# Reordered feed-forward units and sums in a fused attention and mixer kernel

## The chip, the cores and the metric

The kernel runs on one core of one Trainium2 chip. The metric is the device time of one execution in microseconds. The core has five engines with a queue each, all in order: TensorE (PE; its weight loads are PEld), VectorE (DVE), ScalarE (ACT), GpSimd (POOL) and SyncE (SP, which here only issues DMAs). Semaphores tie them together: an instruction that waits holds up all that stands behind it on its engine.

## The reference

The input is four batches of 8 heads, 768 positions and 64 channels. The attention keeps the first 8 positions and a band of 96, with a linear bias by distance; a low-rank token mixer and a feed-forward network follow.

```python
scores = scale * np.matmul(q, k.transpose(0, 1, 3, 2)) + bias        # band of 96 and 8 global columns kept
a = softmax(np.where(keep, scores, -1e9))
x = np.matmul(a, v).transpose(0, 2, 1, 3).reshape(B, S, H * D)       # 4 x 768 x 512
xt = x.transpose(0, 2, 1)
u = x + (xt @ U @ V).transpose(0, 2, 1)                              # U 768 x 32, V 32 x 768
return u + np.maximum(u @ w_ch1, 0.0) @ w_ch2                        # w_ch1 512 x 2048, w_ch2 2048 x 512
```

## The kernel before

**Attention blocks.** A block `i` handles two heads of one batch: batch `i // 4`, head pair `i % 4`, blocks 0 to 15. Its steps are the scores in three parts (`scores`, L366 and L373; `s_dve` adds the bias on VectorE, L406 and L412, into the single buffer `sp`), two exponentials on ScalarE (`st_E`, L430) and the product with v for each of the two heads (`st_V`, TensorE L443 and L447 into the one bank `ob`, then reciprocal L452 and normalisation L466 on VectorE, then a cast to `x16` on GpSimd, L469). From block 7 on the second and third score parts are computed together ("S12"); the first two use the single two-bank tile `sc`, the third takes two of the three `th` banks. A block's steps for the mixer come one block later: `st_M1` (x by U, L478), `st_MT` (L495, copied by VectorE to `tmp16`, L496), `st_M3` (L532 into `sc`, added to `x_sb` by VectorE, L537, cast by GpSimd, L540) and `st_X`, a DMA transpose on SP's queue that gives a quarter of `uT` (L521).

**Feed-forward units.** A batch has three groups of 256 tokens, each two tiles of 128. An *up unit* is eight matmuls of u by w_ch1 (L646) into a `th` bank and a ReLU on ScalarE (L651). For batch 0 a *down unit* is a quarter of one token tile's product with w_ch2: `mk_down(t, part)`, four matmuls (L681) into a `cps` bank (two banks in all, shared with the products below). Quarter `part` reads rows `4 * part` to `4 * part + 3` of `w2_16`, which are chunk `part` of four loads issued on GpSimd's queue (L230). The first quarter of a tile also adds the low-rank term (L675), the last is followed by the add to `x_sb` on VectorE (L686) and the store, which batch 0 keeps for later. For batches 1 to 3 a group of two tiles is done with seven products of half size in place of eight (`mk_product`, x1 to x4 and y1 to y3, L699, add L704). They need sums: of quarters of w_ch2 (t1 to t4, made once) and of quarters of the ReLU output (s1 to s4, in two halves `k` per group), all of them L570 on VectorE.

**The order.** Everything is in an order written out by hand. From block 4 on, each block has nine places (counted 0 to 8) at which `fill(n)` puts `n` units between the attention steps; the order of one block is: first scores, place 0, V of the block before (first head), place 1, S12, place 2, V (second head), second score part's bias add, place 3 (two units from block 8 on, and in some earlier ones), place 4, M1 and the first exponential, place 5, MT, place 6, M3 and the second exponential, place 7, the `uT` transpose, place 8. `unit` takes ups and downs in turn from the two queues `ups_q` and `downs_q`; while `held` is true no down unit is taken. All 24 up units of batch 0 come before any down unit.

**The sums.** `queue_sum` puts a sum with a due count into `jobs` (s) or `slow` (t). After each unit `fill` takes out one sum that is due (two, if more than four s sums are waiting). `queue_weight_sums` queues the t sums when tile 1 of group 0 begins. A product whose sums aren't out yet takes them out by force (`need`).

Of the kernel before, what the change touches and what calls it, by code (L numbers as in the profile page):

```python
# [20 lines left out]
def kernel(  # L21
# [17 lines left out]
    P = 128  # L39
# [4 lines left out]
    NJC = DFF // P  # L44
    R = moe_U.shape[1]
    NP = H // 2
# [40 lines left out]
    def ps_cps(name):  # L87
        return psum.tile([P, 512], FP32, name=name, tag="cps", bufs=2)

    def ps_th(name, dtype=FP32, cols=512):  # L90
        return psum.tile([P, cols], dtype, name=name, tag="th", bufs=3)
# [26 lines left out]
    def cast_qk(i, *engs):  # L118
        got = []
        for st, nm, eng in zip(staged.pop(i), ("q16", "k16"), engs * 2):  # L120
            st16 = stp.tile([P, NSB, 2, D], FP16, name=nm, tag=nm, bufs=2)
            turn_over = eng.copy if eng is nc.scalar else eng.tensor_copy
            turn_over(st16.rearrange("p n h d -> p h n d"), st)
            got.append(st16)
        cast[i] = got
# [78 lines left out]
    v16w = cst.tile([P, S], FP16, name="v16w")  # L204
# [337 lines left out]
    ups_q, downs_q = deque(), deque()  # L542
# [20 lines left out]
    jobs, slow = deque(), deque()  # L563
# [3 lines left out]
    def queue_sum(name, part, out_, a, b_, op, wait=0):  # L567

        def go():
            nc.vector.tensor_tensor(out_, a, b_, op)  # L570
            have.add((name, part))
        (slow if name[0] == "t" else jobs).append((count[0] + wait, go))
# [25 lines left out]
    def weight(w, j):  # L598
        return tw[w][:, j] if w != "t3" else tw[w][j // 2][:, j % 2]
# [11 lines left out]
    def queue_group(b, g):  # L611
        ts = slice(g * FT, (g + 1) * FT)
        uT, tmp16, x_sb = uTs[b], tmps[b], xs[b]
        n0, n1 = 2 * g, 2 * g + 1
        cell = {}

        split = (b, g) in WG
        follow = (b, g + 1) if g + 1 < NFG else (b + 1, 0)
        last = (b, g) == (B - 1, NFG - 1)

        def queue_sums(k):

            h = cell["htr"]
            if k == 0:
                for x in (1, 2, 4):
                    cell[f"s{x}"] = ffp.tile([P, HJ, P], FP16, name=f"s{x}", tag=f"s{x}", bufs=1)
                cell.update(a11=h[:, 0:HJ, 0:P], a12=h[:, HJ:NJC, 0:P],
                            a21=h[:, 0:HJ, P:FT], s3=h[:, 0:HJ, P:FT], a22=h[:, HJ:NJC, P:FT])
            js = slice(k * HJ // 2, (k + 1) * HJ // 2)
            for name, a, b_, op in (  # L630
                ("s1", "a21", "a22", ALU.add), ("s2", "s1", "a11", ALU.subtract),
                ("s4", "a12", "s2", ALU.subtract), ("s3", "a11", "a21", ALU.subtract),
            ):
                queue_sum((name, b, g), k, cell[name][:, js], cell[a][:, js], cell[b_][:, js], op, wait=0 if last else 2)

        def mk_up(at):
            jp = at // 2 + (at % 2) * NJC // 4 if split else at

            def go():
                if jp == 0:  # L640
                    cell["htr"] = ffp.tile([P, NJC, FT], FP16, name="htr", tag="htr", bufs=3)
                hps, done = begun.pop(jp) if jp in begun else (ps_th("hps"), 0)
                for k in range(2):
                    jt = 2 * jp + k
                    for dc in range(done, NDC):
                        nc.tensor.matmul(  # L646
                            hps[:, k * FT:(k + 1) * FT],
                            w1_16[:, dc, jt * P:(jt + 1) * P], uT[:, dc, ts],
                            start=(dc == 0 and k == 0), stop=(dc == NDC - 1 and k == 1),
                        )  # L650
                nc.scalar.activation(  # L651
                    cell["htr"][:, 2 * jp:2 * jp + 2].rearrange("p j t -> p (j t)"), hps, AF.Relu
                )
                if split and at % 4 == 3:
                    queue_sums(at // 4)
            return go

        def store(n, cs=slice(0, DM)):
            def go():
                nc.sync.dma_start(out[b, n * P:(n + 1) * P, cs], x_sb[:, n, cs])  # L660
            if b:
                go()
            else:
                kept.append(go)

        def mk_down(t, part):
            n = 2 * g + t

            def go():
                if (b, g, t, part) == (0, 0, 1, 0):  # L670
                    queue_weight_sums()
                if part == 0:
                    cell["cps"] = ps_cps("cps")
                    if b == 0:
                        nc.tensor.matmul(  # L675
                            cell["cps"], v16w[:, n * P:(n + 1) * P], tmp16,
                            start=True, stop=False,
                        )
                cps, htr = cell["cps"], cell["htr"]
                for jc in range(4 * part, 4 * part + 4):  # L680
                    nc.tensor.matmul(  # L681
                        cps, htr[:, jc, t * P:(t + 1) * P], w2_16[:, jc],
                        start=(b > 0 and jc == 0), stop=(jc == NJC - 1),
                    )
                if part == NJC // 4 - 1:
                    nc.vector.tensor_tensor(x_sb[:, n], cps, x_sb[:, n], ALU.add)  # L686
                    store(n)
            return go

        def mk_product(bank, half, a, w, dst, first=False, done=None):  # L690

            def go():
                if bank not in cell:
                    cell[bank] = ps_cps(bank)
                need(*(((a, b, g), k) for k in range(2) if a[0] == "s"))
                need(*((w, k) for k in range(4 if w == "t3" else 2) if w[0] == "t"))
                ps = cell[bank][:, half]
                for j in range(HJ):
                    nc.tensor.matmul(  # L699
                        ps, cell[a][:, j], weight(w, j), start=(first and j == 0),  # L700
                        stop=(done is not None and j == HJ - 1), skip_group_check=True,
                    )
                n, cs = dst
                nc.vector.tensor_tensor(x_sb[:, n, cs], ps, x_sb[:, n, cs], ALU.add)  # L704
                for what in done or ():
                    store(*what)
            return go

        if b:
            for at in range(NJC // 2):  # L710
                ups_q.append((mk_up(at), (b, g)))
        else:
            first_ups.append([(mk_up(at), (b, g)) for at in range(NJC // 2)])
        if split:
            x1 = mk_product("cx", lo, "a11", "b11", (n0, lo), first=True)
            x2 = mk_product("cx", lo, "s2", "t2", (n0, hi_))
            x3 = mk_product("cx", lo, "s3", "t3", (n1, hi_), done=[(n1, hi_)] if last else None)
            x4 = mk_product("cx", lo, "a22", "t4", (n1, lo), done=[(n1, lo)] if last else [(n1,)])
            y1 = mk_product("cy", lo, "a12", "b21", (n0, lo), first=True)
            y2 = mk_product("cy", hi_, "s1", "t1", (n1, hi_))  # L720
            y3 = mk_product("cy", hi_, "s4", "b22", (n0, hi_), done=[(n0,)])
            for made in (x1, y1, x2, y2, x3, y3, x4):
                downs_q.append((made, (b, g)))
        else:
            for t in range(2):
                for part in range(NJC // 4):
                    downs_q.append((mk_down(t, part), (b, g)))

    ahead, held, kept = [0], [True], deque()

    def fill(n):
        for _ in range(n):
            unit()
            count[0] += 1
            for _ in range(2 if len(jobs) > 4 else 1):
                for queue in (jobs, slow):
                    if queue and queue[0][0] < count[0]:
                        queue.popleft()[1]()
                        break
# [79 lines left out]
    for i in range(NP, NPAIR + 2):  # L819
        b, hp = divmod(i, NP)  # L820
        live = i < NPAIR
        units = iter(
            (0, 1, 1, 2, 1, 1, 1, 1, 1) if i == NP
            else (0, 1, 1, 1, 1, 1, 1, 1, 1) if i + 1 < NPE
            else (1, 1, 1, 2, 1, 1, 1, 1, 1)
        )
# [62 lines left out]
        if live:  # L889
            st_E(i, 0)  # L890
            if i < NPE:
                st_P(i)
        fill(next(units))
        if i >= NPE:
            for _ in range(min(2, len(kept))):
                kept.popleft()()
# [14 lines left out]
            st_X(i - 1)  # L911
        if NPE <= i + 2 < NPE + 2:
            cast_qk(i + 2, nc.gpsimd)
        fill(next(units))
    while ups_q or downs_q:
        fill(1)
# [36 lines left out]
```

## Time and profile before

| | |
|---|---|
| median of 3 runs | 233.32 us (231.82 to 234.01) |
| the profiled execution | 231.37 us |
| its span, first to last instruction | 229.6 us |
| mean granted TensorE clock | 0.998 |
| TensorE busy | 219.3 us (96%) |
| VectorE busy | 158.6 us (69%) |
| ScalarE busy | 125.9 us (55%) |
| GpSimd busy | 70.7 us (31%) |
| L646, up matmuls | 756 x 273 ns |
| L681, down matmuls of batch 0 | 96 x 379 ns |
| L570, weight sums of 128x1024 | 6, most of them 0.68 us |
| w loads, issue to landing | 8.6 us median |

Times in the trace are counted from the start of the span. A matmul's row shows its duration with the pipeline's fill and drain, so that one matmul's time overlaps the next one's: eight L646 matmuls of 273 ns take 0.87 us together. A line of the timeline shows start, duration, engine, line, operation, what it writes and reads, shape and count; what stands in brackets is the idle time of the engine before it, and what ended it. A line of the waits shows who waited for whom, total us, times, and the longest. A window's row shows, for PE, PEld, DVE, ACT and POOL in this order, busy us and the number of instructions, then granted clock and DMA.

### The profile page before, as it was taken

The numbers are of one execution on the slowest core, as the hardware profiler recorded it, in microseconds if no ns is written. First come the engines' busy times: TensorE is split into PE (matmuls) and PEld (weight loads), VectorE is DVE, ScalarE is ACT, GpSimd is POOL, SyncE is SP. The second block draws the span as 40 slices with busy tenths as digits, with TensorE's granted clock in tenths as the row PEclk, the third lists the DMA queues.
The fourth block names the chain that finished last, engine by engine and source line by source line (L and its number), as shares of the span: only waits on it lengthen the run. The fifth ranks groups of instructions, "written<-read, shape, count | busy, mean of one in ns | idle before, by whom it ended". The sixth has DMA issues, their size and how long they took to land.

```text
span 229.6 us, 5883 instructions
## 1 busy us (share of the span) xinstructions
PE 219.3 (96%) x2418; PEld 172.0 (75%) x2420; DVE 158.6 (69%) x346; ACT 125.9 (55%) x196; POOL 70.7 (31%) x115
## 2 busy tenths in 40 slices
PE   7889999999989999998999989999999999999993
PEld 2446678788644546886888868888989888888882
DVE  3688775749586979597979887979764444444452
ACT  6677857685705253958485847392732433333320
POOL 6398637297543423131313131313111000000000
PEclk9999999999999999999999999999999999999999
DMA  6999999989998979999999993751321202010022
GB/s 203 280 291 237 267 221 246 303 159 179 193 170 188 201 184 238 219 232 217 215 245 174 261 178 97 129 174 30 92 67 34 94 0 94 0 69 26 8 86 93
DMA packets 86563, 36.68 MB, mean 160 GB/s; under 512 B 74152, under 2 KB 83592, under 8 KB 86536
## 3 DMA queue, kind: packets, MB, share of 16 engines
q1 hardware_dynamic: 81480, 32.01, 57.5%
q0 software_dynamic: 5056, 4.29, 12.5%
q8 instruction: 19, 0.31, 0.6%
q14 instruction: 8, 0.07, 0.1%
HBM read 27.46 MB, written 6.29 MB: 147 GB/s over the span
## 4 chain that ended last, share of the span: by engine, by line
PE 67%; DVE 11%; DMA 10%; ACT 5%; POOL 4%; issue 1%; SPq 1%; ACTq 0%
PE hps L646 25%; PE cx L699 13%; PE cy L699 10%; PE cps L681 8%; DMA w<-in_moe_w_ch_dram 6%; DMA vst<-in_v_dram 3%; DVE sp L412 3%; PE sc L366 2%; ACT ep L430 2%; PE ob L447 2%; DVE x_sb L466 1%; PE sc L532 1%; PE tp L254 1%; PE ob L443 1%; DVE x_sb L704 1%
## 5 line engine op out<-in xcount | busy, mean ns | idle before, releaser
L646 PE MATMUL hps<-uT,w 128*128 128x256 f16 x756 | 95.5, 273 | 0.2 <-ACT htr L651 0.2
L651 ACT ACTIVATE htr<-hps 128x512 f16<-128x512 f32 x96 | 56.4, 599 | 60.8 <-PE hps L646 60.6
L646 PEld LDWEIGHTS <-w 128*128 128x128 f16 x756 | 71.0, 98 | 9.6 <-issue 0.3
L412 DVE SCALAR_TENSOR_TENSOR sp<-sc,relcat 128x1024 f32<-128x1024 f32 (+1 forms) x27 | 32.1, 1189 | 8.0 <-ACT ep L430 4.3
L430 ACT ACTIVATE ep<-sp 128x1408 f16<-128x1408 f32 x24 | 33.2, 1383 | 0.0
L699 PEld LDWEIGHTS <-htr 128*128 128x128 f16 x288 | 27.7, 98 | 3.4
L704 DVE TENSOR_TENSOR x_sb<-cx,x_sb 128x256 f32<-128x256 f32 x36 | 15.2, 422 | 19.3 <-PE cx L699 18.6
L469 POOL CAST x<-x_sb 128x384 f16<-128x384 f32 x27 | 14.1, 522 | 46.6 <-DVE x_sb L466 43.6
L681 PE MATMUL cps<-w,htr 128*128 128x512 f16 x96 | 23.6, 379 | 1.1 <-DMA w<-in_moe_w_ch_dram 1.1
L540 POOL CAST x<-x_sb 128x768 f16<-128x768 f32 x12 | 11.0, 914 | 43.2 <-DVE x_sb L537 43.2
L699 PEld LDWEIGHTS <-s 128*128 128x128 f16 x216 | 20.2, 98 | 4.3 <-DVE s L570 2.0
L704 DVE TENSOR_TENSOR x_sb<-cy,x_sb 128x256 f32<-128x256 f32 x27 | 11.4, 422 | 12.5 <-PE cy L699 12.3
L466 DVE TENSOR_TENSOR x_sb<-ob,rcp 128x384 f32<-128x384 f32 x30 | 16.7, 558 | 1.0
L366 PEld LDWEIGHTS <-kT 64*128 64x128 f16 x192 | 8.5, 93 | 11.4 <-issue 10.1
L447 PE MATMUL ob<-v,ep 128*128 128x65 f16 x192 | 16.6, 193 | 0.0
L366 PE MATMUL sc<-qT,kT 64*128 64x128 f16 x192 | 15.7, 220 | 0.3 <-DVE x_sb L537 0.2
L681 PEld LDWEIGHTS <-htr 128*128 128x128 f16 x96 | 8.6, 97 | 9.4 <-issue 1.2
L447 PEld LDWEIGHTS <-ep 128*128 128x128 f16 x192 | 13.9, 98 | 2.3 <-issue 0.5
L443 PE MATMUL ob<-vA,ep 128*128 128x65 f16 x160 | 14.4, 194 | 0.4 <-DVE vA L316 0.2
L537 DVE TENSOR_TENSOR x_sb<-sc,x_sb 128x768 f32<-128x768 f32 x12 | 11.5, 956 | 4.6 <-PE sc L532 4.6
L142 POOL CAST v<-vst 128x768 f16<-128x768 f32 x16 | 13.4, 838 | 3.8 <-DMA vst<-in_v_dram 3.8
L373 PE MATMUL sc<-qT,kA 64*128 64x128 f16 x160 | 13.2, 216 | 0.3
(110 smaller groups left out, 320.1 us busy)
## 6 DMA issues: line engine op xcount, KB each, us to landing
qst<-in_q_dram SPq DMA_DIRECT2D x16, 384.0 KB, 5.4
kst<-in_k_dram SPq DMA_DIRECT2D x16, 384.0 KB, 6.4
vst<-in_v_dram SPq DMA_DIRECT2D x16, 384.0 KB, 4.1
out_dram<-x_sb SPq DMA_DIRECT2D x23, 256.0 KB, 3.3
w<-in_moe_w_ch_dram POOLq DMA_DIRECT2D x8, 512.0 KB, 8.6
vA<-v SPq DMA_DIRECT2D x8, 152.3 KB, 4.1
out_dram<-x_sb SPq DMA_DIRECT2D x2, 128.0 KB
uT<-x SPq DMA_TRANSPOSE x12, 3.1
```

Of the source, the lines that this page charges most:

```text
L366: nc.tensor.matmul(scs[hi][:, o:o + P], kT[r, kb * P:(kb + 1) * P], qT[r, kb * P:(kb + 1) * P], start=(o == 0 and not on_pe), stop=(o + P ...
L412: nc.vector.scalar_tensor_tensor(out=sps[i][:, :, c0:c0 + tot], in0=both[:, :, 0:tot], scalar=qk_scale / slope[2 * (i % NP)], in1=relfs[c0 ...
L430: nc.scalar.activation(eps[i][:, hi], sps[i][:, hi], AF.Exp, scale=slope[2 * (i % NP)])
L443: nc.tensor.matmul(ob[:, qi], ep[:, OF[qi - 1]:OF[qi - 1] + P], vA[:, qi - 1, hi], start=True, stop=False,)
L447: nc.tensor.matmul(ob[:, qi], ep[:, DG[qi]:DG[qi] + P], vt[:, qi, hi], start=(qi == 0), stop=True,)
L466: nc.vector.tensor_tensor(xo, ob[:, :, 0:D], rb, ALU.mult)
L469: nc.gpsimd.tensor_copy(x16, xo)
L646: nc.tensor.matmul(hps[:, k * FT:(k + 1) * FT], w1_16[:, dc, jt * P:(jt + 1) * P], uT[:, dc, ts], start=(dc == 0 and k == 0), stop=(dc == ...
L651: nc.scalar.activation(cell["htr"][:, 2 * jp:2 * jp + 2].rearrange("p j t -> p (j t)"), hps, AF.Relu)
L681: nc.tensor.matmul(cps, htr[:, jc, t * P:(t + 1) * P], w2_16[:, jc], start=(b > 0 and jc == 0), stop=(jc == NJC - 1),)
L699: nc.tensor.matmul(ps, cell[a][:, j], weight(w, j), start=(first and j == 0), stop=(done is not None and j == HJ - 1), skip_group_check=True,)
L704: nc.vector.tensor_tensor(x_sb[:, n, cs], ps, x_sb[:, n, cs], ALU.add)
```

## The change

- Token tiles of a group have an accumulator each (`cell[t]`), so that both can be open.
- In group (0, 0) the fourth quarters of both tiles are moved behind the third quarters of both: (0,0), (0,1), (0,2), (1,0), (1,1), (1,2), (0,3), (1,3) as (tile, quarter).
- `held` is cleared ahead of place 8 of block 6, not at the start of block 7.
- The second-half s sums (k = 1) are due one unit after they are queued, not two; those of the first half stay at two, and the last group's at none.
- From block 5 on, place 5 lets out no sum; the next unit may take out one more.

```diff
@@ queue_sums
-                queue_sum((name, b, g), k, ..., op, wait=0 if last else 2)
+                queue_sum((name, b, g), k, ..., op, wait=0 if last else 2 - k)
@@ mk_down
                 if part == 0:
-                    cell["cps"] = ps_cps("cps")
+                    cell[t] = ps_cps("cps")
                     if b == 0:
                         nc.tensor.matmul(
-                            cell["cps"], v16w[:, n * P:(n + 1) * P], tmp16,
+                            cell[t], v16w[:, n * P:(n + 1) * P], tmp16,
                             start=True, stop=False,
                         )
-                cps, htr = cell["cps"], cell["htr"]
+                cps, htr = cell[t], cell["htr"]
@@ queue_group
-            for t in range(2):
-                for part in range(NJC // 4):
-                    downs_q.append((mk_down(t, part), (b, g)))
+            order = [(t, part) for t in range(2) for part in range(NJC // 4)]
+            if (b, g) == (0, 0):
+                order.sort(key=lambda u: u[1] == NJC // 4 - 1)
+            for u in order:
+                downs_q.append((mk_down(*u), (b, g)))
@@ fill
-    def fill(n):
+    owed = [0]
+
+    def fill(n, quiet=False):
         for _ in range(n):
             unit()
             count[0] += 1
-            for _ in range(2 if len(jobs) > 4 else 1):
+            pops = owed[0] + (2 if len(jobs) > 4 else 1)
+            owed[0] = 1 if quiet else 0
+            for _ in range(0 if quiet else pops):
                 for queue in (jobs, slow):
                     if queue and queue[0][0] < count[0]:
                         queue.popleft()[1]()
@@ the loop over the blocks, place 5
-        fill(next(units))
+        fill(next(units), quiet=i > NP)
@@ the loop over the blocks, place 8
+        held[0] = i < NP + 2
         fill(next(units))
```

More of the change, by code (lines that the diff above doesn't have):

```diff
@@ L633, in queue_sums @@
             ):
-                queue_sum((name, b, g), k, cell[name][:, js], cell[a][:, js], cell[b_][:, js], op, wait=0 if last else 2)
+                queue_sum((name, b, g), k, cell[name][:, js], cell[a][:, js], cell[b_][:, js], op, wait=0 if last else 2 - k)
         def mk_up(at):
```

## The prediction

> **What bounds the kernel now.** Read the engine table first, then who TensorE waited for, then the timeline around each wait.
>
> ```profile
> span 229.6 us, 5883 instructions
> PE 219.3 (96%) x2418; PEld 172.0 (75%) x2420; DVE 158.6 (69%) x346; ACT 125.9 (55%) x196; POOL 70.7 (31%) x115
> ...
> PE cx L699 <- DVE s L570: 1.5, 2, 1.0
> ...
> PE cps L681 <- DMA w<-in_moe_w_ch_dram: 1.1, 1, 1.1
> ...
> PE sc L366 <- DVE x_sb L537: 0.2, 1, 0.2
> PE hps L646 <- ACT htr L651: 0.2, 1, 0.2
> ```
>
> TensorE is busy 219.3 of 229.6 us, and the change neither adds nor removes a matmul. It can win only what TensorE idles in the middle. The waits above (total, times, longest) are all there are between 33 us and the end, and the change touches the neighbourhood of each. The timeline puts them at 60.5, 66.2, 100.4, 104.2 and 137.6 us:
>
> ```profile
> 60.51 0.23 PE L366 MATMUL sc<-qT,kT 64*128 64x128 f16 x2 [0.17 <-DVE x_sb L537]
> ...
> 64.91 0.19 PE L447 MATMUL ob<-v,ep 128*128 128x65 f16 x1
> 66.21 1.02 PE L681 MATMUL cps<-w,htr 128*128 128x512 f16 x4 [1.12 <-DMA w<-in_moe_w_ch_dram]
> ...
> 136.01 0.60 PE L699 MATMUL cx<-t,s 128*128 128x256 f16 x4
> 137.56 0.61 PE L699 MATMUL cx<-t,s 128*128 128x256 f16 x4 [0.96 <-DVE s L570]
> ```
>
> Recorded idle understates the loss, because the drain of the last matmul counts as busy. From issue to issue: the V step before the weight wait issues its last matmul at 64.91 (0.03 each), the next starts at 66.21, so 1.27 is lost, not 1.12. The half product at 136.01 issues four matmuls at 0.109 (eight take 0.87 in the chain), is through at 136.45 and goes on at 137.56: 1.11. In the same way 60.51 costs 0.34 (the up unit from 59.30 is through at 60.17), 104.22 costs 0.65 (from 103.13 + 0.44) and 100.36 costs 0.34 (98.81 + 0.87 + 0.34 for V). **All five: 0.34 + 1.27 + 0.34 + 0.65 + 1.11 = 3.7 us.** That is the ceiling.
>
> **The change, part by part.** I write (i, k) for place k, counted from 0, of attention block i.
>
> *Down units one place sooner.* Walking the two queues by their rule, place (6, 8) is empty before: the 24 up units of batch 0 are done and downs are held. It now takes token tile 0's first quarter: 0.22 for L675 and 0.87 for four L681 matmuls, from 60.17 to 61.26. The scores behind it (L366) needed the L537 result, there at 60.46: that wait goes, gain 0.34. Every later unit stands one place earlier among the attention steps; the units' total is the same, so the tail after the last place loses one.
>
> *Third quarters before fourths.* Quarter q needs chunk q of w2. The issues at 48.01, 48.75, 51.03 and 51.69 landed 7.4, 10.7, 11.8 and 14.5 later: 55.4, 59.4, 62.8 and 66.2. The new order reaches quarters 0, 1, 2 of tile 0 at 60.4, 61.6 and 62.85 (61.26 + 0.38 scores + 0.87 + 0.34 V), so chunk 2 is there by a hair: cost 0, up to 0.3. Then scores 0.5, tile 1's quarter 0 (1.09), V (0.34) and quarters 1 and 2 (1.73) put the fourth quarter at 67.4, 1.2 after its chunk. Gain 1.27. The price is that both cps banks are open at once. Group 1's first unit, at 69.3, needs tile 0's bank, freed by the L686 add (0.69). VectorE reaches it at about 68.45 (two 0.65 weight sums, V's normalisation and the 1.13 score pass stand ahead) and is through at 69.14. Cost 0; if one more 0.65 sum stood ahead, 0.5.
>
> *Where the weight sums now fall.* They start at (7, 2), not (7, 3), so t2's first half stands on VectorE ahead of the residual add L537 of block 6:
>
> ```profile
> 71.76 0.95 DVE L537 TENSOR_TENSOR x_sb<-sc,x_sb 128x768 f32<-128x768 f32 x1
> 72.62 0.68 DVE L570 TENSOR_TENSOR t<-w,t 128x1024 f16<-128x1024 f16 x1
> ...
> L570 DVE TENSOR_TENSOR t<-w,t x4: 681/682/1100, 72.6 to 88.9; 128x1024 f16<-128x1024 f16 x4
> ...
> 86.54 1.28 SPq L521 DMA_TRANSPOSE uT<-x  x1
> ```
>
> That sum can't start before the kA copy, which waits for a transpose landing near 70.8; so the add runs 71.65 to 72.6, as before, while TensorE wants block 8's scores at 72.5 and they need the bank the add reads. Cost 0.2 (0 to 0.6).
>
> The slow sum, 1.10, ran from 74.97 beside Pool's k cast (74.71 to 75.53). The other three took 0.68. The Trainium skill, SBUF — State Buffer, "Who interferes with whom", says that a VectorE instruction with both inputs in SBUF contends with a GpSimd instruction that reads SBUF. By that rule the second t2 half, now due at about 72.5 beside Pool's x cast, would take 1.10 and leave a gain 0.4 smaller than the sum below; the trace agrees for the one pair, but the sum at 72.62 ran 0.68 although the cast began at 72.77. I take 0.68.
>
> *Batch 1's transposed input.* TensorE reaches the first batch-1 up unit at 89.92 now, and after at 89.92 - 1.6 (the two gains so far) + 0.2 = 88.5; I allow 0.2 for the gaps of a few hundredths between steps and say 88.3. Its fourth matmul (+0.33, 88.63) reads the L521 transpose above, issued at 86.54. Transposes of that line landed 3.1 after issue in the median, 4.3 at most. The transpose is the end of a chain: V of block 7, Pool's casts, SP's vA copies at 80.71, two loads, two stores. VectorE's backlog at that V is smaller after (tile 2's add and t2's second half are already out), and SP is free from 79.6, so the chain moves up by 1.1 to 85.45: landing 88.55. I take 0.1; with the slowest landing 1.1.
>
> *ReLU sums.* In block 10 the ups are a place earlier and the second-half sums are due one unit earlier (wait 2 - k). s2's second half is emitted at (10, 2), ahead of the second V and the 1.13 score pass, not behind them at (10, 3). The waits at 104.22 (0.65) and, since L651 of the last up now stands ahead of the k cast that waited for its load, at 100.36 (0.34) go. What is late next is the M1 matmul, which needs Pool's cast of V's output: margin about 0.1 after, 0.5 before. Cost 0.1 (0 to 0.5).
>
> In block 13 the product x2 moves up as well, to (13, 3) right behind V, so there is less time. Counting from block 13's first score: x1 is through at 2.42; on VectorE its add runs to 2.95, s1 to 3.28, two L406 passes to 4.25, y1's add to 4.6, s2 to 5.0. TensorE wants s2's second half at 4.68. Of 1.11 lost, 0.4 stays (0.2 to 0.8).
>
> *Quiet places.* Place 5 lets out no sum, the next one more: this keeps a 0.42 sum from standing ahead of the tmp cast (L496, 0.29) that M3 waits for. Nothing recorded waits there; 0. After block 17, units follow each other at 0.87 with sums of 0.42: no wait there before, none after. Stores for later tiles move one place up on SP, once past a transpose; its margin of 1.1 us covers one 0.7 issue.
>
> **Sum.** 3.7 - (0 + 0 + 0.2 + 0.1 + 0.1 + 0.4) = **2.9 us**. Extremes: all costs at the upper end (0.3 + 0.5 + 0.6 + 1.1 + 0.5 + 0.8 = 3.8) make it 0.1 slower; none makes it 3.7 faster. Against the profiled execution, 231.37 (span 229.6 and 1.77 around it, which stays), that is 228.5. The median of the runs shown is 233.32; I carry the difference over: 233.32 - 2.9 = **230.4**. The runs differ by 2.2 us among themselves; if it is late w2 chunks that do that, the gain there is much the same: with chunks 2 and 3 both 2 us late, the old order loses 3.3 and the new one 1.9 at quarter 2, after which quarter 3 is covered.
>
> **Rivals.**
> *The waits come back elsewhere (chance 0.26).* The same in-order VectorE feeds everything, and it is full:
>
> ```profile
> 73.40:84.60 11.20, 11.20 (x99) 5.69 (x99) 9.58 (x18) 4.89 (x6) 4.42 (x7) 1.00 0.87 191
> ...
> 95.80:107.00 11.20, 10.43 (x130) 8.70 (x130) 9.95 (x22) 8.69 (x14) 2.19 (x4) 1.00 0.96 223
> ```
>
> The third busy time is VectorE's: 86% and 89% of these blocks. With half of the upper ends of the costs (1.9) the gain is 1.8, with all it is nil: 231.5 to 233.5, within 1%. For it: three margins above are 0.1 or less. Against it: each is a different wait.
>
> *VectorE falls behind for good (chance 0.12).* The single ob bank ties V of one head to the normalisation of the other. If the earlier sums leave VectorE one weight sum (0.65) behind from block 7 on, TensorE waits that long in each of the blocks 7 to 15: nine times 0.65 is 5.9, less 3.7 is 2.2 slower, about 235.5. It decides from 0.41 per block (3.7 / 9). Against it: 1.6 and 1.25 us of slack per block in the two rows; a backlog of 0.65 is gone within one block.
>
> *The change doesn't do what it says*: chunk 3 later than 67.4, or x2 in block 13 no better. Losing either leaves 1.6 or 2.2 of gain; it lies in the first rival.
>
> **Numbers.** The forecast has the rest, 0.62. One per cent, 2.3 us, is about what a measurement of this kernel can tell from no change. The range runs from 228.2 (all 3.7, and 1.4 for the runs' own scatter) to 233.0 (most of the first rival) and leaves out the slower one. Faster by over 1% 0.62, within 1% 0.26, slower by over 1% 0.12.
>
> **What would show it.** After the change: no L681 wait on w, or one of under 0.3 at quarter 2; the first L681 near 60.4, ahead of the scores; t2 ahead of L537 near 71; a short wait of L366 on L537 near 72.5; no x2 wait in block 10 and one of 0.2 to 0.4 recorded in block 13. It is wrong if TensorE then waits for uT near 88.5 by over 1 us, or if VectorE's idle in blocks 8 to 12 disappears.

## The result and the profile after

The changed kernel takes 229.75 us in the median of 22 runs, the kernel before 231.11 in the median of 22 runs of its own; the ratio is 0.9942 with a 95% interval of 0.9921 to 0.9963. That is 1.3 us faster, 0.6%, and within the 1% that the prediction called no change. Five of the changed kernel's 22 executions ran at a granted clock of 0.993 or less (two of them, at 0.56 and 0.66, took 367 and 316 us) and are left out of the ratio. The forecast was 2.9 us, from 233.32 to 230.4, in a range of 228.2 to 233.0. That the time comes within 0.7 us of the forecast is luck: the three runs of the kernel before that the prediction started from were 2.2 us high, the gain was put 1.6 too large, and the two nearly cancel. From 231.11 the same sum gives 228.2 and a range of 226.0 to 230.8, which still holds 229.75.

The page of the changed kernel and who TensorE waited for (total us, times, longest):

```profile
span 227.8 us, 5878 instructions
PE 219.0 (96%) x2420; PEld 171.8 (75%) x2420; DVE 160.1 (70%) x346; ACT 125.7 (55%) x196; POOL 70.3 (31%) x115
...
PE hps L646 <- DMA uT<-x: 1.4, 2, 1.1
...
PE cx L699 <- DVE s L570: 0.2, 1, 0.2
...
PE sc L366 <- DVE x_sb L537: 0.2, 1, 0.2
PE cps L681 <- DMA w<-in_moe_w_ch_dram: 0.2, 1, 0.2
```

The waits on w (1.1) and on s (1.5 in total) are down to 0.2 each, and the one on L651 is gone. In their place stands one that the kernel before did not have: the up matmuls wait for `uT`. The timeline of the changed kernel places all of them:

```profile
62.43 1.02 PE L681 MATMUL cps<-w,htr 128*128 128x512 f16 x4 [0.17 <-DMA w<-in_moe_w_ch_dram]
...
72.50 0.23 PE L366 MATMUL sc<-qT,kT 64*128 64x128 f16 x2 [0.22 <-DVE x_sb L537]
...
88.24 0.49 PE L646 MATMUL hps<-uT,w 128*128 128x256 f16 x3
88.99 2.45 PE L646 MATMUL hps<-uT,w 128*128 128x256 f16 x21 [0.26 <-DMA uT<-x]
...
133.86 0.61 PE L699 MATMUL cx<-t,s 128*128 128x256 f16 x4 [0.24 <-DVE s L570]
134.30 0.49 PE L646 MATMUL hps<-uT,w 128*128 128x256 f16 x3
135.92 0.71 PE L646 MATMUL hps<-uT,w 128*128 128x256 f16 x5 [1.13 <-DMA uT<-x]
```

The 62.43 wait is quarter 2, the 72.50 wait block 8's first scores, 133.86 the product x2 of block 13. At 88.24 and at 134.30 three matmuls of the first up unit of a batch run, and the fourth, which reads the last quarter of `uT`, waits: 0.42 and 1.29 lost from issue to issue (the step to the fourth matmul less the 0.11 that one takes).

**How to compare two profiles here.** The start of the last batch-0 up unit, ahead of everything that the change moves, lies at 59.30 us in the profile before and at 58.51 in the one after: 0.8 of the 1.8 between the two spans comes from code that is the same. So the runs below are compared from that instruction (L646, 8 matmuls) to the last product (L699), which all kernels have. The way is cut in two at batch 1's first up unit; the last column is what the fourth up matmul of a batch lost to `uT` in the second part, from issue to issue:

| kernel | last batch-0 up | last product | from one to the other | up to batch 1 | from there | of it lost to `uT` |
|---|---|---|---|---|---|---|
| before | 59.30 | 224.89 | 165.6 | 30.62 | 134.97 | 0 |
| changed | 58.51 | 223.07 | 164.6 | 29.73 | 134.83 | 1.71 |
| changed, second profile | 58.90 | 223.59 | 164.7 | 29.12 | 135.57 | 2.69 |
| tile order alone | 59.22 | 224.55 | 165.3 | 30.38 | 134.95 | 0 |
| early place alone | 59.05 | 226.70 | 167.7 | 30.83 | 136.82 | 0.19 |
| sums alone | 58.17 | 223.60 | 165.4 | 30.42 | 135.01 | 0 |
| order and early place | 59.33 | 228.02 | 168.7 | 29.71 | 138.98 | 0.76 |
| changed, store of place 7 behind the transpose | 59.41 | 223.05 | 163.6 | 29.11 | 134.53 | 1.65 |
| changed, all stores behind | 59.26 | 221.26 | 162.0 | 29.11 | 132.89 | 0 |
| the same, second profile | 59.21 | 221.50 | 162.3 | 29.41 | 132.89 | 0 |
| changed, kept stores alone behind | 61.38 | 224.36 | 163.0 | 29.11 | 133.87 | 1.00 |
| changed, stores of places 5 to 7 alone behind | 64.03 | 226.29 | 162.3 | 29.11 | 133.16 | 0.27 |
| before, all stores behind | 57.96 | 223.31 | 165.4 | 30.39 | 134.96 | 0 |

The rows with stores moved belong to the second half of the experiments.

### The profile page after: what moved, and what is told of

It is laid out like the page before. It is cut to its first block, busy times and chain, and to the rows that moved or that the text cites. A ratio compares the mean times of both kernels' runs of the same rounds, so it can differ in the third digit from the quotient of the medians.

```text
span 227.8 us, 5878 instructions
## 1 busy us (share of the span) xinstructions
PE 219.0 (96%) x2420; PEld 171.8 (75%) x2420; DVE 160.1 (70%) x346; ACT 125.7 (55%) x196; POOL 70.3 (31%) x115
## 4 chain that ended last, share of the span: by engine, by line
PE 70%; DMA 12%; DVE 10%; POOL 3%; ACT 2%; issue 2%; SPq 0%; DVEq 0%
PE hps L646 28%; PE cx L699 13%; PE cy L699 10%; DMA w<-in_moe_w_ch_dram 5%; PE cps L681 4%; DMA uT<-x 4%; PE sc L366 3%; PE tp L254 2%; DVE sp L412 2%; PE ob L447 2%; DMA kst<-in_k_dram 2%; PE ob L443 2%; DMA kT<-k 1%; PE sc L373 1%; PE sc L532 1%
## 5 line engine op out<-in xcount | busy, mean ns | idle before, releaser
L646 PE MATMUL hps<-uT,w 128*128 128x256 f16 x756 | 95.3, 273 | 1.4 <-DMA uT<-x 1.4
L651 ACT ACTIVATE htr<-hps 128x512 f16<-128x512 f32 x96 | 56.4, 599 | 58.4 <-PE hps L646 58.4
L646 PEld LDWEIGHTS <-w 128*128 128x128 f16 x756 | 71.2, 98 | 11.0 <-issue 1.9
L699 PEld LDWEIGHTS <-htr 128*128 128x128 f16 x288 | 27.3, 98 | 3.1
L681 PE MATMUL cps<-w,htr 128*128 128x512 f16 x96 | 23.9, 379 | 0.2 <-DMA w<-in_moe_w_ch_dram 0.2
L540 POOL CAST x<-x_sb 128x768 f16<-128x768 f32 x12 | 10.5, 872 | 42.4 <-DVE x_sb L537 42.4
L699 PEld LDWEIGHTS <-s 128*128 128x128 f16 x216 | 20.3, 98 | 3.2 <-DVE s L570 0.5
L447 PEld LDWEIGHTS <-ep 128*128 128x128 f16 x192 | 13.8, 98 | 2.0 <-issue 0.3
L681 PEld LDWEIGHTS <-htr 128*128 128x128 f16 x96 | 8.5, 97 | 8.5 <-issue 0.3
L537 DVE TENSOR_TENSOR x_sb<-sc,x_sb 128x768 f32<-128x768 f32 x12 | 11.5, 955 | 3.5 <-PE sc L532 3.0
```

Source lines behind the costliest of these rows:

```text
L447: nc.tensor.matmul(ob[:, qi], ep[:, DG[qi]:DG[qi] + P], vt[:, qi, hi], start=(qi == 0), stop=True,)
L646: nc.tensor.matmul(hps[:, k * FT:(k + 1) * FT], w1_16[:, dc, jt * P:(jt + 1) * P], uT[:, dc, ts], start=(dc == 0 and k == 0), stop=(dc == ...
L651: nc.scalar.activation(cell["htr"][:, 2 * jp:2 * jp + 2].rearrange("p j t -> p (j t)"), hps, AF.Relu)
L681: nc.tensor.matmul(cps, htr[:, jc, t * P:(t + 1) * P], w2_16[:, jc], start=(b > 0 and jc == 0), stop=(jc == NJC - 1),)
L699: nc.tensor.matmul(ps, cell[a][:, j], weight(w, j), start=(first and j == 0), stop=(done is not None and j == HJ - 1), skip_group_check=True,)
```

## The experiments

**The parts, one at a time.** First the tile order alone, on the kernel before:

```diff
+            if (b, g) == (0, 0):
+                order.sort(key=lambda u: u[1] == NJC // 4 - 1)      # and cell[t] in place of cell["cps"]
```

> The kernel before with the tile order alone (third quarters of both tiles ahead of the fourths). Theory: quarter 3 of tile 0 is reached near 67.9, behind chunk 3's landing at 66.2, so the wait of L681 on w (1.12) goes whole and the four other waits stay (0.2, 0.2, 0.5, 1.0): 1.3 gained, ratio 0.9945. Rival (a new wait takes its place: the cps bank or VectorE): a wait of L675 or L366 of 0.5 or more near 69 to 73, ratio 0.997 or above.

Measured: 1.0004 (0.9976 to 1.0033), no gain that the interval shows. The wait on w is gone, as the theory had it, but the rival was right about the rest. TensorE's timeline in this run:

```profile
69.91 0.49 PE L532 MATMUL sc<-tmp,v16w 128*128 128x128 f16 x6 [0.16 <-DVE tmp L496]
...
73.00 0.23 PE L366 MATMUL sc<-qT,kT 64*128 64x128 f16 x2 [0.65 <-DVE x_sb L537]
...
103.89 0.61 PE L699 MATMUL cx<-t,s 128*128 128x256 f16 x4 [0.81 <-DVE s L570]
```

and VectorE's, which says why block 8's scores can't start before 73:

```profile
70.71 0.18 DVE L340 COPY kA<-kT 128x40 f16<-128x40 f16 x1 [0.85 <-DMA kT<-k]
70.80 0.68 DVE L686 TENSOR_TENSOR x_sb<-cps,x_sb 128x512 f32<-128x512 f32 x1
71.39 0.68 DVE L570 TENSOR_TENSOR t<-w,t 128x1024 f16<-128x1024 f16 x1
71.99 0.95 DVE L537 TENSOR_TENSOR x_sb<-sc,x_sb 128x768 f32<-128x768 f32 x1
```

The kA copy stands in VectorE's queue and waits for a transpose that lands near 70.7 whatever TensorE does (70.8 before and after). The tile's add, a weight sum and the L537 add are behind it, and the scores need the bank that L537 reads. So there is a second floor right behind the w2 wait: of 1.27 saved, 0.2 is left when block 8's scores start (73.00 - 59.22 = 13.8 after the last up, 14.0 before), and 0.3 at the end.

The early place alone:

```diff
+        held[0] = i < NP + 2
         fill(next(units))
```

> The kernel before with the first down unit one place sooner, tile order and sums as before. Theory: the wait at 60.5 goes (0.34 from issue to issue), but quarter 3 is reached near 64.2 and waits 2.0 for chunk 3, where it was 1.3; x2 comes sooner too and waits longer for its sum in block 13. Ratio 1.002 (1.000 to 1.006). Rival (coming sooner is a gain by itself): ratio 0.9985 or less.

Measured: 1.0148 (1.0094 to 1.0202), slower, and more than expected. TensorE's waits in this run:

```profile
PE cx L699 <- DVE s L570: 3.4, 2, 2.4
PE cps L681 <- DMA w<-in_moe_w_ch_dram: 1.3, 1, 1.3
```

In its timeline the waits for s are 1.03 in block 10 and 2.40 in block 13, against 0.49 and 0.96 before: the products come one place sooner, their sums don't. The wait on w grew less than expected, as chunk 3 landed at 65.4 here (51.4 + 14.0), not 66.2.

The sums alone:

```diff
-  wait=0 if last else 2)
+  wait=0 if last else 2 - k)
-        fill(next(units))
+        fill(next(units), quiet=i > NP)                             # place 5; with owed in fill
```

> The kernel before with the sums let out elsewhere alone (second halves due a unit sooner, quiet places). Theory: the waits on w2 and at 60.5 stay as they are; the wait for s in block 10 (0.49) goes and that in block 13 (0.96) falls to about 0.4: 1.0 to 1.2 gained, ratio 0.9955. Rival (what is gained there is lost to the transpose or to other VectorE work): new waits of the same size in the same blocks and ratio 0.998 or above.

Measured: 1.0004 (0.9975 to 1.0034); the rival, again. The wait for s in block 10 went, that in block 13 fell only to 0.82, and block 8's, 12's and 15's first scores now wait for L537:

```profile
PE sc L366 <- DVE x_sb L537: 1.2, 4, 0.5
...
PE cx L699 <- DVE s L570: 0.8, 1, 0.8
PE cps L681 <- DMA w<-in_moe_w_ch_dram: 0.3, 1, 0.3
```

The sums that were let out behind L537 now stand ahead of it. VectorE of this run in block 12, where before L537 came first and s1's second half after it:

```profile
115.83 0.43 DVE L570 TENSOR_TENSOR s<-htr 128x512 f16<-128x512 f16 x1
116.29 0.43 DVE L570 TENSOR_TENSOR s<-s,htr 128x512 f16<-128x512 f16 x1
116.64 0.95 DVE L537 TENSOR_TENSOR x_sb<-sc,x_sb 128x768 f32<-128x768 f32 x1
```

Chunk 3 landed sooner in this execution (64.3), hence only 0.3 on w. The 0.2 that an up unit waited for L651 near 100 was 0.3 here.

**Two parts of three.** The changed kernel without its sums part:

```diff
-  wait=0 if last else 2 - k)
+  wait=0 if last else 2)
-        fill(next(units), quiet=i > NP)
+        fill(next(units), quiet=False)
```

> The changed kernel with the second-half sums due after two units again and no quiet places: only the tile order and the early first down unit. Theory (each part pays its own wait, and the early place needs the earlier sums): the w2 wait is 0.2 or less, L366's wait on L537 near 60.5 gone: 1.4 gained there; but x2 comes a place sooner in blocks 10 and 13 with the sums as late as before, so TensorE waits for s about 0.7 in block 10 and 1.5 to 2 in block 13, against 0.5 and 1.0 before. Ratio 0.998 (0.995 to 1.001). Rival (the sums' places matter nothing): waits for s at 0.5 to 1.0 in total and ratio 0.994.

Measured: 1.0111 (1.0075 to 1.0148). The theory's waits for s are there and larger than expected; the ratio missed the range given. The granted clock was 0.990 in this profile (0.79 between 138 and 146 us), so part of its 168.7 in the table is that, and a wait for `uT` of 0.60 in block 9 is in it too; the two waits for s are not:

```profile
104.16 0.61 PE L699 MATMUL cx<-t,s 128*128 128x256 f16 x4 [1.03 <-DVE s L570]
...
138.22 0.61 PE L699 MATMUL cx<-t,s 128*128 128x256 f16 x4 [2.40 <-DVE s L570]
```

Its VectorE shows the mechanism in block 13. s2's second half (137.59) is behind V's normalisation and the score pass:

```profile
135.43 0.41 DVE L570 TENSOR_TENSOR s<-htr 128x512 f16<-128x512 f16 x1
135.76 0.19 DVE L452 RECIPROCAL rcp<-ob 128x6 f32<-128x6 f32 x1
135.98 0.56 DVE L466 TENSOR_TENSOR x_sb<-ob,rcp 128x384 f32<-128x384 f32 x1
136.46 1.21 DVE L412 SCALAR_TENSOR_TENSOR sp<-sc,relcat 128x1024 f32<-128x1024 f32 x1
137.59 0.58 DVE L570 TENSOR_TENSOR s<-s,htr 128x512 f16<-128x512 f16 x1
```

In the changed kernel the same sum is ahead of them:

```profile
133.06 0.41 DVE L704 TENSOR_TENSOR x_sb<-cy,x_sb 128x256 f32<-128x256 f32 x1
133.39 0.41 DVE L570 TENSOR_TENSOR s<-s,htr 128x512 f16<-128x512 f16 x1
133.94 0.56 DVE L466 TENSOR_TENSOR x_sb<-ob,rcp 128x384 f32<-128x384 f32 x1
134.41 1.21 DVE L412 SCALAR_TENSOR_TENSOR sp<-sc,relcat 128x1024 f32<-128x1024 f32 x1
```

So no part by itself shows a gain: order and sums are each worth 0.2 to 0.3 us from up to product, with ratios that can't be told from 1, and the early place costs. The early place gives TensorE one more unit to do ahead of block 8's scores, which covers the floor that cost the tile order its gain; the early place needs the earlier sums, or x2 waits; and the tile order lets the early downs run without chunk 3. The two other pairs, sums with the order or with the early place, were not run.

**Where the rest of the gain went.** Theory: it is in the `uT` wait. Moving the down units one place up has moved the products' stores one place up too. In block 12 a second store now stands ahead of the transpose on SP. SP's queue there in the kernel before, whose cast L540 ended at 130.68, so that the store didn't hold the transpose up:

```profile
128.98 1.43 SPq L660 DMA_DIRECT2D out_dram<-x_sb  x1
130.71 1.29 SPq L521 DMA_TRANSPOSE uT<-x  x1
132.10 0.53 SPq L660 DMA_DIRECT2D out_dram<-x_sb  x1
```

And in the changed kernel:

```profile
127.67 0.45 SPq L111 DMA_DIRECT2D qst<-in_q_dram  x1
128.17 0.74 SPq L111 DMA_DIRECT2D kst<-in_k_dram  x1
129.01 2.15 SPq L660 DMA_DIRECT2D out_dram<-x_sb  x2
131.25 1.29 SPq L521 DMA_TRANSPOSE uT<-x  x1
```

The transpose's input was ready before that: L540's cast ran from 128.29 to 129.12. First a control, the changed kernel once more:

> The changed kernel once more, as the control of this call. Ratio to the kernel before 0.994 (0.992 to 0.996), and in its profile the wait of L646 on uT near 136 us (1.13 in the profile of after, from a transpose issued at 131.25 that landed near 135.9). If that wait is an accident of one execution, it is under 0.3 here.

Measured: 0.9962 (0.9932 to 0.9992). The wait is no accident; it is larger here:

```profile
PE hps L646 <- DMA uT<-x: 2.4, 2, 1.6
```

Then the store of place 7 alone issued behind the transpose:

```diff
+        defer[0] = True                # while set, a store goes to put_off
         fill(next(units))              # place 7
+        defer[0] = False
...
             st_X(i - 1)
+        while put_off:
+            put_off.popleft()()
```

> The changed kernel, but an output store that falls on place 7 of a block is issued behind the L521 transpose of that block, not ahead of it; TensorE's order is untouched. Theory (the store ahead of the transpose cost the gain): in block 12 the transpose is issued one store (1.07) sooner, near 130.2, lands near 134.8, and the wait of L646 on uT near 136 falls from 1.13 to 0.1; ratio 0.990. Rival (the transpose lands late because of what else is in flight, whatever stands ahead of it): the wait stays near 1.1, ratio 0.994.

Measured: 0.9924 (0.989 to 0.9958), which lies between the two and tells nothing apart. The wait in block 13 is gone, but not for the reason given: the transpose was issued at 131.52, not 130.2, because the one store left ahead of it began 0.7 later and held SP for 1.68, not for half of 2.15, and TensorE came late itself, having waited 1.49 for `uT` in block 9 in this execution. Then all the stores:

```diff
+        defer[0] = True
         fill(next(units), quiet=i > NP)            # place 5
...
-                kept.popleft()()
+                put_off.append(kept.popleft())
...                                                # places 6 and 7
+        defer[0] = False
...
             st_X(i - 1)
+        while put_off:
+            put_off.popleft()()
```

> As the run before, but all stores of places 5 to 7, and batch 0's kept stores of blocks 8 to 10, are issued behind that block's L521 transpose. Theory: the transposes of blocks 8 and 12 are issued up to 2 us sooner (block 8 near 84.2 when its cast is there, block 12 near 129.2), both uT waits (0.26 and 1.13) go, ratio 0.988 to 0.989. Rival (landing set by other traffic): ratio 0.994, waits as in after.

Measured: 0.986 (0.9803 to 0.9917). There is no wait for `uT` anywhere; SP's queue in block 12:

```profile
127.06 0.70 SPq L111 DMA_DIRECT2D kst<-in_k_dram  x1
128.62 1.69 SPq L521 DMA_TRANSPOSE uT<-x  x1
130.41 0.99 SPq L661 DMA_DIRECT2D out_dram<-x_sb  x2
```

From the last batch-0 up to the last product it takes 162.0, 2.6 and 2.7 less than the two profiles of the changed kernel, though only SP's order differs. Once more, beside its parts:

> The version with all stores of places 5 to 7 and the kept stores behind the transpose, again, beside its parts. Theory: no wait of L646 on uT, span from the last batch-0 up unit to the last matmul 162.0 as in its first profile (164.6 to 164.7 in the two of the changed kernel, 165.6 before), ratio 0.986 (0.983 to 0.989). If the first result was luck of one set of executions: 0.991 or above.

Measured: 0.9853 (0.9809 to 0.9897), 162.3 from up to product, again without a `uT` wait. This version beats both kernels, the changed one by about 0.9% (0.9853 against 0.9942; the first time 0.986 against 0.9962 for the changed kernel run beside it, with intervals that don't overlap).

Only batch 0's kept stores behind the transpose:

> The changed kernel with only batch 0's kept stores (blocks 8 to 10) behind the transpose. Theory: the uT wait in block 9 (0.3 to 1.5 in the profiles that have it) goes, the one in block 13 stays and grows by what was saved ahead of it (1.6 to 2.6), since the transposes of batch 2 come when they came. Ratio 0.994 (0.991 to 0.996): one wait alone taken away gains little. Rival (the waits are independent): ratio 0.990.

Measured: 0.9915 (0.9884 to 0.9945), which covers both numbers. Block 9's wait is gone and block 13's is there, 0.83 (1.00 from issue to issue); it did not grow as the theory said. SP's chain of block 12 moved up along with TensorE's work, by 1.6 (the transpose is issued 71.2 after the last batch-0 up, 72.7 in the changed kernel), so the two waits are not independent and not simply one for the other either.

Only the stores of places 5 to 7:

> The changed kernel with only the output stores that fall on places 5 to 7 behind the transpose, the kept stores as in the change. Theory: the uT wait in block 9 stays (0.3 to 1.5), the one in block 13 is gone, ratio 0.990 (0.988 to 0.993).

Measured: 0.989 (0.984 to 0.994), as expected. Its page lists no `uT` wait, but the one in block 9 is there, too short to be listed: the fourth up matmul began at 93.73, 0.27 later than without a wait. The profile's mean clock was 0.993 and TensorE reached batch 1 only at 93.14, yet the lower clock (0.91) lay between 20 and 40 us, ahead of everything that is compared here; from up to product it takes 162.3, as short as with all stores moved.

**What the stores are worth.** The table's last two columns settle it for the part from batch 1 on. The seven profiles of the changed kernel and its four store orders run the same 1463 matmuls there. Take away what each lost to `uT`, and six of them take 132.9; the first profile of the changed kernel takes 133.1. So the order of the stores works through the `uT` waits and through nothing else there. As far as one profile of each part shows, the kept stores set the wait in block 9 and the stores of places 5 to 7 the one in block 13.

Last, the same move in the kernel before:

> The kernel before with the stores behind the transpose as in the best version. It has no uT wait in its profile, so there is nothing to win: waits as before (1.1 on w2, 0.5 and 1.0 on s), ratio 1.000 (0.997 to 1.003). Rival (stores cost the kernel before too, for instance in the landing of loads): ratio 0.995 or less.

Measured: 0.9963 (0.9936 to 0.9991). The waits are as before (0.9 on w, 1.6 on s), but the interval excludes 1.000: something of 0.4% is there that TensorE's waits don't show. From the last up to the last product it takes 165.35 against 165.59 in the profile before, which is 0.1% and lies wholly ahead of batch 1, where the wait on w was 0.2 shorter; from there on the two are alike (134.96 and 134.97). Where the rest is was not traced.

## Why the prediction was right and wrong

**Down units one place sooner: right.** The first L681 ran ahead of the scores and the wait on L537 near 60.5 went. **Third quarters before fourths: right**, with the hair's breadth too: quarter 2 waited 0.33 from issue to issue in the first profile (forecast 0, at most 0.3) and not at all in the second. **The weight sums:** block 8's scores waited 0.22 as recorded (0.39 from issue to issue, forecast 0.2) in the first profile, nothing in the second. These three were forecast to gain 1.4 up to batch 1's first up unit. Measured from the last batch-0 up to that unit, 30.62 before: 29.73 and 29.12 in the changed kernel's two profiles and 29.11 to 29.41 in the five with stores moved, a gain of 0.9 to 1.5.

**ReLU sums: right.** Block 10's waits went (0.99 with the one for the bank) and M1 cost nothing that shows; block 13's x2 waits 0.24 as recorded, 0.41 from issue to issue, forecast 0.4. From block 10's first scores to block 13's M1, with the same units between them, it took 42.21 before and 40.41 in the version without the `uT` waits: 1.80, forecast 1.6.

**Quiet places: put at nothing, and worth more.** The prediction said that nothing recorded waits for the `tmp` cast. The kernel before has two such gaps, in blocks 10 and 16, of 0.12 each, too short to be listed. The one in block 10:

```profile
104.72 1.04 PE L646 MATMUL hps<-uT,w 128*128 128x256 f16 x8
105.88 0.50 PE L532 MATMUL sc<-tmp,v16w 128*128 128x128 f16 x6
...
105.21 0.41 DVE L570 TENSOR_TENSOR htr<-htr 128x512 f16<-128x512 f16 x1
105.54 0.28 DVE L496 CAST tmp<-ob 128x128 f16<-128x128 f32 x1
```

The eight up matmuls are through at 105.59 (0.87), so M3 lost 0.29, with a sum ahead of the cast; block 16 lost 0.28. Both gaps are gone in the changed kernel and with the sums alone, while the versions without quiet places still have two of 0.12 each, some in other blocks. So the ceiling was nearer 4.3 than 3.7.

**The step that failed is the transposed input of batches 1 and 2.** For batch 1 the prediction took the median landing of its row, 3.1, and put the cost at 0.1. The issue was foreseen well, 85.45 against 84.96 (85.75 on the scale of the profile before), but the transposes took 4.0 in both profiles of the changed kernel from issue to the start of the matmul that waited for them (84.96 to 88.99, 85.28 to 89.27; the trace has no landing for these): 0.42 and 0.92 lost. The prediction's sign of being wrong, over 1 us there, did not show in these two, but in the version with place 7's store moved, which is the same up to there, it did: 1.65. For batch 2 it said that a margin of 1.1 us covers one 0.7 issue past which the transpose moves, and gave it no term in the sum. There the two stores held SP for 2.15 and the matmul that waited began 4.7 after the issue: 1.29 lost, and 1.8 in the second profile. Together 1.7 to 2.7 lost against 0.1, which covers the gap between the forecast 2.9 and the measured 1.3. With these waits taken out by SP's order alone, the gain from last up to last product is 3.3 and 3.6 (165.6 to 162.3 and 162.0): about the forecast 2.9 and the 0.6 of the quiet places together.

**The rivals.** What came is a case of the first one, waits that come back elsewhere, at 0.26; but it named VectorE as their source, and it was a DMA queue. VectorE's busy time in the same two windows rose only from 9.58 to 9.83 and from 9.95 to 10.06, and the only wait on it that is listed after block 8 is the 0.24 in block 13, so it did not fall behind for good. The chance of 0.62 for a gain over 1% looks too high: the sum had three margins of 0.1 or less, each with a worse end that the prediction itself allowed, and took the favourable side of each.

**The Trainium skill's rule** of SBUF — State Buffer, "Who interferes with whom", was weighed against the row and left out of the sum. In the changed kernel the second t2 half ran beside Pool's x cast and took 0.68, not 1.10:

```profile
72.36 0.68 DVE L570 TENSOR_TENSOR t<-w,t 128x1024 f16<-128x1024 f16 x1
72.51 1.22 POOL L540 CAST x<-x_sb 128x768 f16<-128x768 f32 x1 [3.73 <-DVE x_sb L537]
```

Pool's cast, from 72.51, took 1.22 where most L540 casts take 0.83. So the contention is there, but in both pairs the one that began second paid: the sum at 74.97 in the kernel before, the cast here. The same section of the Trainium skill has that as "Issue order, not op shape, decides who blocks", and this trace agrees.

## What to carry to other kernels

When a stall is removed, look at once for the next floor behind it, on every queue: here the kT landing stood 4.5 us behind the w2 wait, took back 1.0 of the 1.27 us that the tile order alone had saved, and was covered only by work moved ahead of it. A reordering by places moves everything that is issued with the moved unit, the stores on a DMA queue too; a store that nobody waits for does not belong ahead of a transpose that the bound engine will need. Parts that are each worth nothing, or cost a per cent, can be a gain together, so a part that fails alone is no argument against the whole, nor the whole a sign that each part is sound.

## What the runs showed that was not expected

The start of the kernel scatters more than the change is worth: the last batch-0 up unit, behind identical code, began between 57.96 us (the kernel before with moved stores) and 64.03 (the one with the stores of places 5 to 7 moved, which had the lower clock between 20 and 40 us; 61.38 at full clock, with the kept stores moved), while the way from there to the last product repeated within 0.1 and 0.3 for the two kernels that were profiled twice. What scatters there was not looked into.

The L521 transposes that the late waits hung on took 4.0 to 4.8 us from issue to the matmul that waited (84.96 to 88.99, 131.25 to 135.92, 131.64 to 136.45), where the median of those that the trace gives a landing for is 3.1 in the profile before. Whether the stores issued just ahead of them stretch that, or the loads around them, is open; no run held the issue time and took the neighbours away. A store directly ahead isn't enough by itself: the transpose of block 11 has one such store in both kernels, and landed 3.4 after issue before (120.30 to 123.69) and 5.0 after the change (120.48 to 125.44), where nothing waited for it.
